# First chunk's keys and values as fp32 through POOL's queue, and a new order of the whole kernel

## The chip, the core and the metric

The kernel runs on one core of one Trainium2 chip. Five engines take part: TensorE (PE; matmuls and, through an identity matrix, transposes), VectorE (DVE), ScalarE (ACT), GpSimd (POOL) and SyncE (SP), which here only issues transfers. POOL issues transfers too. Each engine works through its own instructions in the order in which the program has them and waits on semaphores for the others. The metric is the device time of one execution in microseconds.

## What is computed

The reference has two stages. The first is a recurrence over 768 positions for 4 batches of 8 heads, each with a 48 x 48 state; the second a sum of four expert networks, weighted by row-normalised probabilities.

```python
f = 1.0 / (1.0 + np.exp(-f_logit))                     # q, k, v, f_logit: (4, 8, 768, 48)
for t in range(S):
    state = f[:, :, t, :, None] * state + np.einsum('bhd,bhe->bhde', k[:, :, t], v[:, :, t])
    y[:, :, t] = np.einsum('bhd,bhde->bhe', q[:, :, t], state)
x = y.transpose(0, 2, 1, 3).reshape(3072, 384)
p = domain_probs / (domain_probs.sum(-1, keepdims=True) + 1e-09)
for e in range(4):
    out += p[:, e:e + 1] * (np.maximum(x @ w1[e], 0.0) @ w2[e])   # w1: 384 x 1024, w2: 1024 x 384
```

## The kernel before

The 768 positions are cut into six chunks of 128. A chunk goes through the recurrence in its parallel form and then, batch by batch, into the four expert networks. Chunk 0 has no state before it, so it is the short way to the first expert matmul; everything below concerns it.

For each batch b of chunk 0 the steps are these, by the names that the code gives them:

- `gate1`, `gate2` (ScalarE, L334 and L339): log(1 + exp(-f)), the negative logarithm of the gate.
- `cs` and `cq` (TensorE, L351, L355 and L362): its running sums over the positions, by matmuls with triangular matrices.
- `exps` and `expq` (ScalarE, L382, L384 and L387): the exponentials of both sums, for the keys and for the queries.
- `k` and `q` (L397, L394): keys and queries multiplied by them, on VectorE or POOL.
- `tpk`, `tpq` (TensorE, L406) and `ev_tp` (L288): both are transposed and copied out of PSUM.
- `at` (TensorE, L437), `ev_at0` and `ev_at1` (L449 on VectorE with a 0/1 mask, or L445 on ScalarE with `mask1` on POOL, L441): the 128 x 128 products of keys and queries, with the future masked out.
- `y` (TensorE, L464), `ev_y` (L287 or L288): their product with v; `kv` (L470): the state for the next chunk.
- `xt` (TensorE, L490) and `ev_xt`: the transpose that the experts read. The expert matmuls `h` of chunk 0 (L499) follow, four blocks of 128 columns at a time for one batch.

v is needed in bf16 by `y` and `kv` (tile `vb`). In chunk 0 a transfer with a cast, issued on POOL (L293), writes `vb` directly; from chunk 1 on v is loaded as fp32 by SyncE and cast by POOL or ScalarE. Weights are always loaded with a cast, through POOL's queue (L312), in eleven pieces w0 to w10: w0 and w1 are the two halves of expert 0's first matrix. The loads of f, q and k of chunk 0 are issued by SyncE (L299 and L301), one of 192 KB for each batch. Ahead of chunk 1, its first loads of f are tied to the landing of weight pieces (`after(..., ins["w", w_gate])`).

All work is added to a plan as operations (`P.add`) with a cost on each engine, dependencies and buffers. A string of ranks, RANKS, has one number for each operation in the order in which they are added: the program is emitted in the order of these numbers, and a letter behind a number (A, D, P) puts an operation with a choice on ScalarE, VectorE or POOL. The costs and `free_at` in `Plan.run` only serve the choice of buffers; they wait for nothing on the chip. FILLER names operations ahead of which idle matmuls of 512 columns on a spare bank are put (L1156). SEQ is the order of POOL's issues, ORDER that of SyncE's adds, GATE makes an issue of v wait until keys have landed, and BYPOOL names the two masked evictions that ScalarE and POOL share.

Ahead of the plan stands a preparation that each engine runs first: an identity matrix, triangular matrices `Up`, `Wp` and `Ub`, the zeroed padding of tiles `gp`, `qk` and `e`, and the mask `mask01` (L193 to L230).

Of the kernel before, what the change touches and what calls it, by code (L numbers as in the profile page):

```python
# [11 lines left out]
ALU = mybir.AluOpType  # L12
# [79 lines left out]
class Plan:  # L92
# [20 lines left out]
    def run(self):  # L113
# [7 lines left out]
        for o in done:  # L121
            (e, cost), = o.costs.items()
            t = free_at[e]
# [1081 lines left out]
```

## Time and profile before

| | |
|---|---|
| median of three runs | 285.59 us (285.1 to 287.25) |
| the profiled execution | 285.82 us |
| its span in the trace | 284.1 us |
| TensorE busy | 276.0 us of the span, 97% |
| VectorE, ScalarE, POOL busy | 208.7, 178.2, 185.3 us |
| granted clock of TensorE | 1.00 in all stretches but the last |
| moved by the DMA engines | 41.88 MB, 147 GB/s on average |

In the views below, times count from the start of the span. A row of the timeline has start, length, engine, line, operation, output and inputs with their shapes, the number of instructions merged into the row, and in brackets the idle time of the engine before it with what ended it. A row of a table by stretches has the stretch, its length, the busy time of PE, PEld (its weight loads), DVE, ACT and POOL with the number of instructions, then the granted clock, the share of DMA time and GB/s. A row "DMA to landing" has the least, median and greatest time from the issue of a transfer to its landing, for the issues named in the row above it. The ends of matmuls are modelled, so a row of TensorE is a little longer than the time to the next one's start.

### The profile page before, as it was taken

To read this page: it belongs to the slowest core of one execution; us is meant where nothing else is said; L and a number is where in the kernel's file an instruction comes from. 1 tells how busy PE (TensorE), PEld (TensorE's weight loads), DVE (VectorE), ACT (ScalarE), POOL (GpSimd) and SP (SyncE) were. 2 spreads that over 40 slices of the span, in tenths; PEclk is the share of its full clock that TensorE was granted. 3 is DMA by queue.
4 is the path that set the end of the run, shared out by engine and by line. 5 is a ranking of instruction groups with operands and counts; after the bars stand their busy time and mean duration, and the time that the engine had idled before them with its cause. 6 is when DMAs were issued, how large, how long until landed. Compare 5 with 4: busy or idle time off the path is not lost.

```text
span 284.1 us, 8015 instructions
## 1 busy us (share of the span) xinstructions
PE 276.0 (97%) x3228; PEld 241.2 (85%) x3228; DVE 208.7 (73%) x437; ACT 178.2 (63%) x350; POOL 185.3 (65%) x197
## 2 busy tenths in 40 slices
PE   6889999999999999999999999999999999999995
PEld 4678565668788999999998999999999899999995
DVE  5695487797779587769887786686765687857683
ACT  5668235647898848686866867769367456556420
POOL 5799353706699878667729955695656545793761
PEclk9999999999999999999999999999999999999999
DMA  6999999999988999999999999996547015201003
GB/s 156 189 195 205 208 195 200 184 216 181 162 150 159 198 164 208 204 168 184 194 175 207 194 179 218 184 166 124 111 82 160 30 31 76 67 0 59 2 2 111
DMA packets 153688, 41.88 MB, mean 147 GB/s; under 512 B 144028, under 2 KB 152860, under 8 KB 153652
## 3 DMA queue, kind: packets, MB, share of 16 engines
q1 hardware_dynamic: 142404, 34.66, 65.1%
q0 software_dynamic: 11248, 6.72, 16.8%
q8 instruction: 25, 0.41, 0.6%
q14 instruction: 11, 0.09, 0.1%
HBM read 31.51 MB, written 4.72 MB: 128 GB/s over the span
## 4 chain that ended last, share of the span: by engine, by line
PE 84%; DMA 9%; POOL 4%; ACT 1%; DVE 1%; issue 0%; ACTq 0%; POOLq 0%
PE ps_m L646 29%; PE ps_m L531 26%; PE ps_m L574 7%; DMA w_sb<-in_moe_w_dram 7%; PE ps_m L514 6%; PE ps_m L499 4%; PE ps_m L654 2%; DMA f<-in_f_logit_dram 2%; PE ps_m L437 2%; POOL w_sb L312 2%; PE ps_m L464 1%; PE ps_m L460 1%; PE ps_m L347 1%; PE ps_m L470 1%; POOL AT L441 1%; PE ps_m L362 1%
## 5 line engine op out<-in xcount | busy, mean ns | idle before, releaser
L531 PE MATMUL ps_m<-x,w_sb 128*128 128x256 bf16 x672 | 84.3, 273 | 0.0
L531 PEld LDWEIGHTS <-w_sb 128*128 128x128 bf16 x672 | 63.6, 98 | 7.1
L595 ACT ACTIVATE h<-ps_m 128x512 bf16<-128x512 f32 x82 | 46.8, 600 | 24.1 <-PE ps_m L531 23.9
L646 PEld LDWEIGHTS <-S 128*128 128x128 bf16 x576 | 48.2, 98 | 0.8
L673 DVE TENSOR_TENSOR o<-ps_m,o 128x192 f32<-128x192 f32 x91 | 31.1, 353 | 19.1 <-PE ps_m L646 17.3
L646 PEld LDWEIGHTS <-h 128*128 128x128 bf16 x432 | 36.2, 98 | 0.8
L610 POOL TENSOR_TENSOR S<-h 128x1024 bf16<-128x1024 bf16 x14 | 29.7, 2124 | 10.3 <-DVE S L610 6.3
L499 PE MATMUL ps_m<-x,w_sb 128*128 128x128 bf16 (+2 forms) x264 | 35.1, 282 | 0.0
L420 ACT ACTIVATE yb<-ps_m,pn 128x384 bf16<-128x384 f32 x55 | 29.4, 586 | 8.5 <-PE ps_m L464 5.6
L397 POOL TENSOR_TENSOR qk<-q,e 128x384 bf16<-128x384 f32 x18 | 21.6, 1201 | 12.5 <-DVE f L549 3.9
L646 PE MATMUL ps_m<-ts_sb,S 128*128 128x192 bf16 x288 | 29.3, 246 | 0.0
L646 PE MATMUL ps_m<-w_sb,h 128*128 128x192 bf16 x288 | 29.2, 246 | 0.0
L646 PE MATMUL ps_m<-w_sb,S 128*128 128x192 bf16 x288 | 28.7, 246 | 0.0
L499 PEld LDWEIGHTS <-w_sb 128*128 128x128 bf16 x264 | 21.6, 98 | 8.1
L593 DVE TENSOR_SCALAR h<-ps_m 128x512 bf16<-128x512 f32 x30 | 20.6, 688 | 9.6 <-PE ps_m L531 8.5
L453 DVE TENSOR_TENSOR AT<-ps_m,mask 128x512 bf16<-128x512 f32 x40 | 25.6, 682 | 2.1 <-PE ps_m L437 2.0
L510 ACT ACTIVATE h<-ps_m 128x512 bf16<-128x512 f32 x33 | 19.1, 595 | 12.2 <-PE ps_m L499 11.8
L380 ACT ACTIVATE e<-ps_m 128x384 f32<-128x384 f32 x40 | 23.6, 708 | 3.2 <-PE ps_m L347 1.4
L610 POOL TENSOR_TENSOR S<-h,S 128x1024 bf16<-128x1024 bf16 x10 | 21.2, 2124 | 4.5 <-DVE o L673 2.5
L514 PE MATMUL ps_m<-w_sb,h 128*128 128x384 bf16 x128 | 23.9, 326 | 0.0
L585 DVE CUSTOM_DVE_ANT_0 h<-ps_m,QK 128x512 bf16<-128x512 f32 x24 | 16.0, 686 | 5.1 <-PE ps_m L574 1.9
L588 ACT COPY QK<-ps_m 128x512 f32<-128x512 f32 x24 | 13.8, 588 | 8.1 <-PE ps_m L574 5.2
(140 smaller groups left out, 523.3 us busy)
## 6 DMA issues: line engine op xcount, KB each, us to landing
out_dram<-o SPq DMA_DIRECT2D x23, 192.0 KB, 2.5
w_sb<-in_moe_w_dram POOLq DMA_DIRECT2D x5, 768.0 KB, 15.2
k<-in_k_dram SPq DMA_DIRECT2D x10, 384.0 KB, 5.1
q<-in_q_dram SPq DMA_DIRECT2D x10, 384.0 KB, 5.0
v<-in_v_dram SPq DMA_DIRECT2D x10, 384.0 KB, 5.1
f<-in_f_logit_dram SPq DMA_DIRECT2D x9, 384.0 KB, 5.8
w_sb<-in_moe_w_dram POOLq DMA_DIRECT2D x6, 384.0 KB, 8.2
f<-in_f_logit_dram SPq DMA_DIRECT2D x6, 192.0 KB, 4.4
```

The costliest lines, as they stand in the source:

```text
L380: nc.scalar.activation(out=o, in_=i, func=AF.Exp, scale=1.0 if j else -1.0)
L397: return engines[eng].tensor_tensor(out=tl("qk", c, b)[:, j, :, 0:D].rearrange("t (i r) d -> t i r d", r=2), in0=tl("qk"[j], c, b // 2)[:, ...
L420: nc.scalar.activation(out=ys, in_=y, func=AF.Copy, scale=pe)
L453: nc.vector.tensor_tensor(out=tl("AT", c, b)[:, r].rearrange("s i t -> s (i t)"), in0=tl("A", c, b, r).rearrange("s i t -> s (i t)"), in1= ...
L499: nc.tensor.matmul(out=hp(c, e, fc, n0, n1, nf)[:, f], lhsT=w1_sb[:, e, kk, (fc + f) * 128:(fc + f + 1) * 128], rhs=tl("xT", c)[:, kk, n0: ...
L514: nc.tensor.matmul(out=tl("op", c, e, nt)[:, 0:Din], lhsT=tl("h", c, e, half_of(c, nt * T))[:, fc, nt * T:(nt + 1) * T], rhs=w2_sb[:, e, f ...
L531: nc.tensor.matmul(out=out_[:, f], lhsT=w1_sb[:, e, kk, (fc + f) * 128:(fc + f + 1) * 128], rhs=tl("xs", c, hf, p)[:, el, kk, :], start=(k ...
L593: nc.vector.tensor_relu(out=dst, in_=tl("hp", c, hf, p, el, fc))
L595: nc.scalar.activation(out=dst, in_=tl("hp", c, hf, p, el, fc), func=AF.Relu)
L610: return engines[eng].tensor_tensor(out=o, in0=in0, in1=in1, op=op)
L646: nc.tensor.matmul(out=out_, lhsT=lhs[:, f, :], rhs=rhs[:, f, :], start=(first and el == 0 and f == 0), stop=(el == 1 and f == KH - 1), sk ...
L673: nc.vector.tensor_tensor(out=o, in0=src, in1=o, op=ALU.add)
```

## The change

Three things are changed in chunk 0 and in the preparation, and RANKS is another string for the whole kernel.

```diff
     def load(c, nm, b, n):
-        if (c, nm) == (0, "v"):
-            ins[c, nm, b] = nc.gpsimd.dma_start(out=tl("vb", c, b), in_=srcs[nm][c, :, b * H:(b + n) * H, :])
-            if f"v{b}" in GATE:
-                after(ins[c, nm, b], ins[GATE[f"v{b}"]])
+        if c == 0 and nm in "kv":
+            ins[c, nm, b] = nc.gpsimd.dma_start(out=tl(nm, c, b // 2)[:, hh(b, n), :], in_=srcs[nm][c, :, b * H:(b + n) * H, :])
             return
...
-        if x[0] == "v":
-            issued.append(P.add(f"v issue {i}", {"POOL": 0.8}, lambda _, i=i: load(0, "v", i, 1), -600 + 2 * j,
-                                deps=issued[-1:] + gate(x), takes=[("vb", 0, i)], lag=1.2))
+        if x[0] != "w":
+            issued.append(P.add(f"{x[0]} issue {i}", {"POOL": 0.95}, lambda _, i=i, nm=x[0]: load(0, nm, i, 1), -600 + 2 * j,
+                                deps=issued[-1:], takes=[(x[0], 0, i // 2)], lag=1.2))
...
-            vb = ld[0, "v", b] if c == 0 else P.add(f"v {c}.{b}", {"POOL": 0.52, "ACT": 0.54}, one(cast_v), s(4),
+            vb = P.add(f"v {c}.{b}", {"POOL": 0.52, "ACT": 0.54} if c else {"POOL": 0.52, "ACT": 0.54, "DVE": 0.34}, one(cast_v), s(4),
                        deps=[ld[c, "v", b]], takes=[("vb", c, b)], frees=[("v", c, half)])
...
-    nc.gpsimd.memset(Ub, 1.0)
-    nc.gpsimd.affine_select(out=Ub, in_=Ub, compare_op=ALU.is_ge, fill=0.0, base=0, channel_multiplier=-1, pattern=[[1, T]])
+
+    nc.vector.memset(Ub, 1.0)
+
+    def make_ub():
+        return nc.gpsimd.affine_select(out=Ub, in_=Ub, compare_op=ALU.is_ge, fill=0.0, base=0, channel_multiplier=-1, pattern=[[1, T]])
+
...
-        nc.gpsimd.memset(pads["e", i][:, 0:2 * NP * P2].rearrange("t (r d i) -> t r d i", r=2, i=NP)[:, :, D:P2, :], 0.0)
+        nc.vector.memset(pads["e", i][:, 0:2 * NP * P2].rearrange("t (r d i) -> t r d i", r=2, i=NP)[:, :, D:P2, :], 0.0)
     mask01 = const.tile([T, NP * T], BF16)
-    nc.gpsimd.memset(mask01, 1.0)
-    nc.gpsimd.affine_select(
-        out=mask01, in_=mask01, compare_op=ALU.is_ge, fill=0.0,
-        base=0, channel_multiplier=-1, pattern=[[0, NP], [1, T]],
-    )
+
+    nc.vector.memset(mask01, 1.0)
+
+    def make_mask():
+        return nc.gpsimd.affine_select(
+            out=mask01, in_=mask01, compare_op=ALU.is_ge, fill=0.0,
+            base=0, channel_multiplier=-1, pattern=[[0, NP], [1, T]],
+        )
+
...
+    masked = P.add("mask", {"POOL": 0.65}, lambda e: make_mask(), -599)
+    upper = P.add("ub", {"POOL": 0.3}, lambda e: make_ub(), -100)
...
-FILLER = {"cs 0.0": 6, "tpk 0.1": 4}
+FILLER = {"cs 0.0": 6, "y 0.1": 1, "y 0.0": 1}
...
-        free_at = {"DMA": 0.8, "DVE": 5.0, "POOL": 3.5, "ACT": 2.1, "PE": 2.0}
+        free_at = {"DMA": 0.8, "DVE": 6.0, "POOL": 2.9, "ACT": 2.1, "PE": 2.0}
...
-ORDER = "f0 k0 q0 f1 k1 q1 f2 f3 k2 q2 k3 q3"
-SEQ = "v0 v1 v2 w0 v3 w1"
+ORDER = "f0 q0 f1 q1 f2 f3 q2 q3"
+SEQ = "k0 k1 k2 v0 k3 v1 w0 v2 w1 v3"
 BYPOOL = "1.1 2.1"
 VW = (-2000, -480)
-GATE = {"v0": (0, "k", 1), "v1": (0, "k", 2)}
```

Keys and v of chunk 0 go as plain fp32 loads through POOL's queue, v is cast to `vb` by an operation of its own, POOL's part of the preparation ends with `Up` (the fills go to VectorE, the two selections become operations of the plan), and nothing waits by GATE any more. `masked` is a dependency of the evictions of `at`, `upper` of the running sums of later chunks.

What the two strings of ranks make of the first stage, read off for each queue and engine (batch numbers behind the names, "a" and "b" for the halves of batch 3):

| | before | after |
|---|---|---|
| SyncE's loads | f0 f1 k2 f2 k1 k0 q0 q1 q2 f3 k3 q3 probabilities | f0 q0 f1 q1 f2 f3 q2 probabilities q3 |
| POOL | issues of v0 v1 v2 w0 v3; k 2; issues of w1 w2; mask1 of 1; issues of w3 w4 w5; mask1 of 2; issue of w6 | issues of k0 k1 k2 v0 k3 v1 w0; ub; issue of v2; mask; cast v 0; issue of w1; mask1 of 1; issues of v3 w2; mask1 of 2; cast v 2; issues of w3 to w8 |
| ScalarE | gate1 0, gate2 0, gate1 1, gate2 1, exps 0, gate1 2, exps 1, expq 1, gate2 2, expq 0, expq 2, exps 2, gate1 3, gate2 3, ev_at1 1, exps 3, expq 3, ev_y 0 | gate1 0, gate2 0, gate1 1, gate2 1, gate1 2, expq 0, exps 0, gate2 2, expq 1, exps 1, expq 2, exps 2, gate1 3, gate2 3, ev_tp 0, ev_at1 1, cast v 1, expq 3, exps 3, ev_y 1, ev_y 0 |
| VectorE | k 1, k 0, q 0, q 1, ev_tp 0, q 2, ev_tp 1, ev_at0 0, ev_at1 0, ev_at0 1, ev_tp 2, k 3, q 3, ev_kv 0, ev_at0 2 | q 0, k 0, q 1, k 1, q 2, k 2, ev_tp 1, ev_tp 2, ev_at0 1, ev_at1 0, ev_at0 0, q 3, k 3, ev_xt 1, ev_tp 3a, ev_at0 2 |
| TensorE | cs 0, cq 0, cs 1, cq 1, tpk 1, cq 2, tpk 0, cs 2, tpq 0, tpq 1, at 0, tpq 2, at 1, cs 3, cq 3, tpk 2, y 0, kv 0, at 2, xt 0, y 1, tpk 3, tpq 3, probabilities, kv 1, first h (batch 0) | cs 0, cq 0, cq 1, cs 1, cq 2, cs 2, tpk 0, tpq 1, tpq 0, tpk 1, tpq 2, tpk 2, cq 3, at 1, at 0, probabilities, cs 3, at 2, y 1, y 0, kv 0, xt 1, tpq 3, tpk 3, xt 0, first h (batch 1) |

More of the change, by code (lines that the diff above doesn't have):

```diff
@@ L312, in load_w @@
         ins["w", i] = nc.gpsimd.dma_start(out=w[:, e, ks, cols], in_=r[e][:, ks, cols])
-        if f"w{i}" in GATE:
-            after(ins["w", i], ins[GATE[f"w{i}"]])
         if i == w_last:
@@ L689 @@
     issued, late = [], {(0, x[0], int(x[1])): i for i in LATE for x in LATE[i].split()}
-    def gate(x):
-        return [ld[GATE[x]]] if x in GATE else []
     for i, x in enumerate(ORDER.split()):
-        add_load(0, x[0], int(x[1]), 1, -1000 + i)
+        add_load(0, x[0], int(x[1]), 1, -1000 + i, deps=[o for o in P.ops[-1:] if i])
     every = slice(0, None)
@@ L704 @@
         i = int(x[1:])
-        if x[0] == "v":
-            issued.append(P.add(f"v issue {i}", {"POOL": 0.8}, lambda _, i=i: load(0, "v", i, 1), -600 + 2 * j,
-                                deps=issued[-1:] + gate(x), takes=[("vb", 0, i)], lag=1.2))
-            ld[0, "v", i] = P.add(f"ld v0.{i}", {"DMA": 1.45}, lambda _: None, VW[0] + j, deps=issued[-1:] + fifo[-1:], lag=2.0)
-            fifo.append(ld[0, "v", i])
+        if x[0] != "w":
+            issued.append(P.add(f"{x[0]} issue {i}", {"POOL": 0.95}, lambda _, i=i, nm=x[0]: load(0, nm, i, 1), -600 + 2 * j,
+                                deps=issued[-1:], takes=[(x[0], 0, i // 2)], lag=1.2))
+            ld[0, x[0], i] = P.add(f"ld {x[0]}0.{i}", {"DMA": 0.6}, lambda _: None, VW[0] + j, deps=issued[-1:] + fifo[-1:], lag=2.0)
+            fifo.append(ld[0, x[0], i])
             continue
@@ L717 @@
         iss = P.add(f"w issue {i}", {"POOL": 0.8}, lambda _, i=i, x=(e, which, ks, cols): load_w(i, *x),
-                    -600 + 2 * j, deps=issued[-1:] + gate(x) + ([ld[1, "k", 0]] if i == w_last else []), lag=1.5)
+                    -600 + 2 * j, deps=issued[-1:] + ([ld[1, "k", 0]] if i == w_last else []), lag=1.5)
         op = P.add(f"w {i}", {"DMA": 1.95 if i < 6 else 4.05}, lambda _: None, -400 if i == w_last else (VW[1] if i < 2 else -480) + j, deps=[iss] + fifo[-1:], lag=1.0)
@@ L754, in attention @@
             cs = P.add(f"cs {c}.{b}", {"PE": 0.165 if c else 0.45}, on(pe_cs), s(0),
-                       deps=[G[b]], takes=[pt_("cs")], lag=0.2, frees=[("gp", c, half)])
+                       deps=[G[b]] + ([upper] if c else []), takes=[pt_("cs")], lag=0.2, frees=[("gp", c, half)])
             ex = P.add(f"exps {c}.{b}", {"ACT": 1.19 if c else 0.56}, on(exps), s(0) + 0.1, deps=[cs],
@@ L794, in attention @@
             at, vb = AT_[b], VB[b]
-            eA = [P.add(f"ev_at{r} {c}.{b}", {"ACT": 0.735} if c == 0 and f"{b}.{r}" in BYPOOL.split() else {"DVE": 0.685 if c else 0.73}, one(ev_at, r), s(7) + 0.1 + 0.1 * r, deps=[at],
+            eA = [P.add(f"ev_at{r} {c}.{b}", {"ACT": 0.735} if c == 0 and f"{b}.{r}" in BYPOOL.split() else {"DVE": 0.685 if c else 0.73}, one(ev_at, r), s(7) + 0.1 + 0.1 * r, deps=[at, masked],
                         takes=[("AT", c, b)], frees=[pt_("A", r)]) for r in range(2)]
```

123 rows, old and new, of the table RANKS are left out of this document.

## The prediction

> **What bounds the kernel now.** The page comes first, then TensorE's busy time in stretches of 10 us, because a mean over the span does not say where the little idle time lies.
>
> ```profile
> span 284.1 us, 8015 instructions
> PE 276.0 (97%) x3228; PEld 241.2 (85%) x3228; DVE 208.7 (73%) x437; ACT 178.2 (63%) x350; POOL 185.3 (65%) x197
> ```
> ```profile
> 0.00:10.00 10.00, 7.78 (x40) 4.65 (x41) 5.24 (x16) 6.18 (x13) 5.86 (x20) 1.00 0.77 177
> 10.00:20.00 10.00, 7.92 (x129) 6.64 (x128) 8.22 (x17) 6.37 (x15) 9.33 (x11) 1.00 1.57 180
> 20.00:30.00 10.00, 10.00 (x143) 7.91 (x138) 5.14 (x15) 7.29 (x14) 9.54 (x20) 1.00 1.25 207
> ...
> 40.00:50.00 10.00, 9.32 (x75) 6.29 (x73) 7.64 (x17) 4.78 (x8) 4.50 (x3) 1.00 1.13 196
> ...
> 280.00:284.10 4.10, 0.99 (x13) 0.77 (x10) 0.78 (x3) 0.00 (x0) 0.00 (x0) 0.97 0.38 135
> ```
> The second number of each row is TensorE's busy time. Of its 8.1 us of idleness 2.2 and 2.1 lie in the first 20 us, 0.7 between 40 and 50, and 3.1 behind its last matmul. From 20 us on TensorE is the bound, so the change is worth what it does to the moment at which the unbroken stretch begins, and to the one wait at about 48 us. Busy is not useful, though: the timeline of TensorE shows fillers and slow matmuls in the first stage.
>
> ```profile
> 4.96 0.80 PE L351 MATMUL ps_m<-gp,Up 128*128 128x192 bf16 x4 [0.70 <-POOL mask L220]
> ...
> 7.68 1.92 PE L1156 MATMUL ps_m<-S 128*128 128x512 bf16 x4
> ...
> 10.85 0.49 PE L351 MATMUL ps_m<-gp,Up 128*128 128x192 bf16 x4
> ...
> 18.89 0.83 PE L499 MATMUL ps_m<-x,w_sb 128*128 128x128 bf16 x12
> ```
> L1156 are the fillers, which fill waits. Four equal matmuls of L351 take 0.80 us at 4.96 and 0.49 at 10.85, so TensorE reaches its speed only at about 10.8 us. The first expert matmul (L499) starts at 18.89, and from there the end of the kernel is a sum of matmuls.
>
> **Part by part.** The first question is what ScalarE gets when. Its rows, with SyncE's issues and the size of one load:
>
> ```profile
> 4.39 0.53 ACT L339 ACTIVATE gp<-f 128x384 bf16<-128x384 f32 x1
> ...
> 6.70 0.52 ACT L334 ACTIVATE f<-f 128x384 f32<-128x384 f32 x1 [0.27 <-DMA f<-in_f_logit_dram]
> ...
> 7.99 0.49 ACT L387 ACTIVATE e<-ps_m 128x384 f32<-128x384 f32 x1 [0.17 <-PE ps_m L362]
> 8.38 0.52 ACT L339 ACTIVATE gp<-f 128x384 bf16<-128x384 f32 x1
> 8.79 0.48 ACT L387 ACTIVATE e<-ps_m 128x384 f32<-128x384 f32 x1
> ```
> ```profile
> 2.92 0.61 SPq L299 DMA_DIRECT2D f<-in_f_logit_dram  x1
> ...
> 3.57 1.45 SPq L301 DMA_DIRECT2D k<-in_k_dram  x2
> ```
> ```profile
> w_sb<-in_moe_w_dram POOLq DMA_DIRECT2D x6, 384.0 KB, 8.2
> f<-in_f_logit_dram SPq DMA_DIRECT2D x6, 192.0 KB, 4.4
> ```
> ```profile
> 4.00:10.00 6.00, 5.30 (x35) 3.77 (x34) 2.62 (x5) 4.73 (x12) 2.99 (x5) 1.00 1.04 232
> 10.00:18.00 8.00, 5.92 (x100) 4.88 (x97) 6.80 (x13) 5.29 (x13) 7.33 (x8) 1.00 1.60 177
> ```
> *SyncE's queue.* The ranks put its loads as f0, q0, f1, q1, f2, f3, q2, the probabilities, q3. In ScalarE's new order the third gate (f2) stands ahead of every exponential (gate1 of 2 has rank 21, the first exponential 22), so nothing of batch 0 goes on before f2 has landed; call that time T. Before, f2 was fourth and landed at 6.70. As fifth it comes one load later: 0.65 us by the spacing of the issues (2.92 to 3.57), 0.85 by 192 KB at 232 GB/s, so about 7.4. Now the keys come through POOL's queue beside it. None of k0 ahead of f2's bytes gives T = 7.4, all of k0 and k1 ahead gives 7.4 + 1.7 = 9.1. I take 8.2, one load's worth, since POOL can start k0 only after its masks, as follows.
>
> ```profile
> 1.76 1.04 POOL L202 TENSOR_SCALAR_AFFINE_SELECT Up<-par 128x128 bf16<-128x128 bf16 x4 [0.39 <-DVE par L197]
> ...
> 4.29 0.63 POOL L220 TENSOR_SCALAR_AFFINE_SELECT mask<-mask 128x512 bf16<-128x512 bf16 x1
> ...
> 7.87 2.85 POOL L293 DMA_DIRECT2D vb<-in_v_dram  x3 [2.94 <-DMA k<-in_k_dram]
> ```
> The Trainium skill (DMA: Bandwidth & Descriptors, "Issuing engines are not separate DMA queues") speaks against the split: transfers started by several engines run on the same 16 DMA engines and interleave, and only issue time is saved. By that rule the 1.5 loads that SyncE's queue still has at that point (q1 and f2) let 1.5 loads of keys pass, T would be 7.4 + 1.3 = 8.7, and the result 0.5 us above my sum; the rows lean to it, with 232 GB/s from one queue (4 to 10 us) and 177 from two (10 to 18, where one of them casts).
>
> *From T to the first expert matmul.* ScalarE starts an instruction about 0.4 us after the one before (7.99, 8.38, 8.79). Gate, expq 0, exps 0, second gate of batch 2: the fourth starts at T + 1.25 and ends at T + 1.8. The cumulative sums cq 2 and cs 2 follow on TensorE, twice 0.80 at the slow speed, and exps 2 takes 0.5: T + 3.9. The rest is VectorE's order, k 2, the evictions of transposes 1 and 2, three masked evictions, q 3, k 3, the eviction of x 1:
>
> ```profile
> 4.59 0.36 DVE L230 CAST ident<-ident 24x24 f32<-24x24 bf16 x1
> ...
> 13.37 1.97 DVE L449 TENSOR_TENSOR AT<-ps_m,mask 128x512 bf16<-128x512 f32 x3
> ...
> 15.24 0.67 DVE L288 COPY QK<-ps_m 112x1024 bf16<-112x1024 bf16 x1
> ...
> 16.29 0.56 DVE L394 TENSOR_TENSOR qk<-q,e 128x384 bf16<-128x384 f32 x1
> ...
> 19.93 0.36 DVE L288 COPY x<-ps_m 128x384 bf16<-128x384 bf16 x1
> ```
> That is 3 x 0.56 + 2 x 0.67 + 1.97 + 0.36 = 5.35, so T + 9.25 if VectorE never waited. It does wait for transposes and attention products on TensorE; I allow 0.4 with TensorE at speed and 1.2 without (the 0.80 against 0.49 above, over some four such groups), and take 0.75. The first expert matmul starts at T + 10.0 = 18.2, against 18.89: 0.7 us gained, with bounds of T + 9.65 = 17.05 (1.85 gained) and 9.1 + 10.45 = 19.55 (0.65 lost). The work done on TensorE by then is the same as before but for kv 1 (one group), which I leave out.
>
> *The weights.* What must cover this is w0.
>
> ```profile
> L312 POOL DMA_DIRECT2D w_sb<-in_moe_w_dram x1: 768/768/768, 10.7 to 10.7; - x1
> ...
> DMA to landing us min/median/max: 8.0/8.0/8.0
> ```
> ```profile
> L312 POOL DMA_DIRECT2D w_sb<-in_moe_w_dram x1: 809/809/809, 14.0 to 14.0; - x1
> ...
> DMA to landing us min/median/max: 7.3/7.3/7.3
> ```
> ```profile
> L293 POOL DMA_DIRECT2D vb<-in_v_dram x4: 893/918/1077, 7.9 to 11.4; - x4
> ...
> DMA to landing us min/median/max: 6.1/7.1/8.4
> ```
> Those are w0, w1 and the four loads of v. Before, w0 landed at 10.7 + 8.0 = 18.7, with the first expert matmul right behind it, and w1 at 14.0 + 7.3 = 21.3. The four cast loads of v landed between 7.9 + 6.1 = 14.0 and 11.4 + 8.4 = 19.8; with w0 among them (384 KB at 207 GB/s, 1.9 us), three took 5.8 - 1.9 = 3.9 us, 1.3 each, where a plain load took 0.85. In the new order fourteen plain loads are ahead of w0; with f0 in at about 3.8 (before the first gate, which ended where the second begins, 4.39), 13 x 0.85 + 1.9 puts w0 at 16.8 and w1, behind v2, at 19.5. So w0 has 1.4 us in hand. All later weights should come some 1.3 us earlier too (four times 0.45 of cast saved, less a gap while v3 and w2 stand behind the mask of batch 1 in POOL's order).
>
> *The wait at 48 us.*
>
> ```profile
> 47.24 0.84 ACT L334 ACTIVATE f<-f 128x768 f32<-128x768 f32 x1 [1.47 <-DMA f<-in_f_logit_dram]
> ```
> The gate of the second chunk waits for a load that is itself tied to a weight's landing. TensorE arrives 0.7 us earlier, the load up to 1.3, so up to 0.6 of the 0.7 us of idleness goes; I take half, 0.35.
>
> *What costs nothing.* POOL's mask work ended at 4.29 + 0.63 = 4.92, and the first sum waited for it, but the gate that it also needs ended at 4.39 + 0.53 = 4.92: no gain. VectorE takes over the fills; its preparation ended at 4.95 and its first product now comes at T + 0.9, a cover of 4 us. The masks are made on POOL behind eight issues of 0.95 (2.85 / 3), by about 11.5, and are needed at T + 6. Two casts of v lie on POOL (before, it idled 2.9 us there) and two on ScalarE, which VectorE's order outlasts. They add waits: behind the cast of v0 on POOL stand w1's issue and the mask of batch 1, behind that of v1 on ScalarE expq 3 and the evictions of y 1 and y 0; v0 and v1 should be in at 3.8 + 9 x 0.85 = 11.5 and 3.8 + 13 x 0.85 = 14.9, about when POOL and ScalarE (T + 7) come to them. The removed fillers filled waits; their only price would be the clock, below.
>
> Sum: the profiled execution took 285.82 (span 284.1, the rest around it; the median of the runs shown is 285.59). 285.82 - 0.7 - 0.35 = **284.8 us**.
>
> **Rivals.**
> *Both queues together carry more* (T = 7.4, TensorE at speed): start at 17.05, 1.85 gained, and the wait at 48 gone, 0.7: 283.2. For it: v's cast loads made the mixed stage slow. Against it: one queue alone already moved 232 GB/s.
> *The clock stays down.* Before, TensorE sped up at 10.8 after work without a break since 4.96, in which the four fillers at 7.68 (1.92 us) closed a gap. These fillers go, and between the sums of batch 1 (about 8) and those of batch 2 (T + 1.8 = 10) nothing runs. If TensorE then needs the same 5.9 us of dense work, and finds it only among the expert matmuls, half of it is lost, 2.9, and the start slips by the other 0.45 of its allowance: 284.8 + 3.35 = 288.2. It decides where the first twelve matmuls of L499 take about 1.5 us in place of 0.83. Against it: sums, transposes and products between T + 1.8 and T + 7 are dense at the low speed and may raise it earlier. The Trainium skill (TensorE: Matmul & The Clock Gate, "What's actually happening") gives a free-running window of about 3.4 us; by that the loss is half of 3.4, and the time 287.0.
> *Packets of POOL's queue stay dear without the cast*, 1.3 us a load: w0 lands at 16.8 + 6 x 0.45 = 19.5 and w1 at 19.5 + 7 x 0.45 = 22.7, 1.4 us later than before, and everything behind it with it: 285.82 + 1.4 = 287.2. It decides from about 1.1 us a load (18.2, where the sum has the first expert matmul). For it: all that the trace shows of v's loads. Against it: the cast goes, and a load then writes what a load of SyncE's writes.
>
> **Chances.** Forecast 0.40, both queues 0.27, clock 0.22, dear packets 0.11. One per cent is about what a measurement here can tell (the three runs span 285.1 to 287.25). Faster by over 1% is under 282.7: the first rival with a little more from the new order elsewhere, 0.18. Slower by over 1% is above 288.4: the clock's upper half, and clock and packets together, 0.22. Within: 0.60. The range runs from 282.5 (the first rival and 0.7 us of order) to 288.7 (the clock and half a microsecond). The forecast's own range, with T half a load off, the wait wholly gone or wholly kept and TensorE's allowance at either end, is 283.7 to 286.0.
>
> **What would show it.** Right: gate1 of f2 at about 8.2 with ScalarE waiting for that load; L499 first at about 18.2 and not waiting for w0; no wait near 48 of over 0.4. Wrong: L499 ended by a wait for a weight (packets), x12 of L499 above 1.2 us (clock), L499 ahead of 17.3 (both queues), or new idle stretches of TensorE after 20 us, which would mean that the new order, not the loads, decides.

## The result, and the profile after

The kernel after took 293.78 us (median of four runs, 293.48 to 294.8), the kernel before on the same chip 285.79 (285.1 to 287.25): a ratio of 1.0279 with a 95% interval of 1.0231 to 1.0326. That is 8 us slower, where the prediction had 284.8 us and a range up to 288.7. Each ratio in this document compares undisturbed runs alone, so it can differ a little from the quotient of the medians beside it.

The page of the kernel after, its first lines, and TensorE's busy time in the first three stretches (the second number of each row):

```profile
span 292.0 us, 8002 instructions
...
PE 278.3 (95%) x3226; PEld 243.1 (83%) x3226; DVE 213.3 (73%) x448; ACT 179.5 (61%) x353; POOL 186.1 (64%) x191
```
```profile
0.00:10.00 10.00, 5.81 (x30) 3.50 (x31) 4.64 (x19) 4.61 (x10) 8.94 (x19) 1.00 0.80 186
10.00:20.00 10.00, 6.28 (x60) 5.39 (x59) 5.00 (x10) 5.06 (x14) 2.44 (x5) 0.84 0.77 157
20.00:30.00 10.00, 9.54 (x157) 8.26 (x157) 7.92 (x19) 6.25 (x16) 7.88 (x11) 0.82 0.91 142
```
From 10 to 20 us TensorE does 60 matmuls, where the kernel before does 129 in the same stretch, and every engine is less busy than before: something outside them is awaited. The chain of waits names it. Here are its longest pieces (start, length, what) in order of time, those of TensorE left out:

```profile
4.96 11.18 DMA q<-in_q_dram
...
54.35 10.55 DMA v<-in_v_dram
...
108.34 2.06 POOL S L615
110.40 3.43 DMA egs<-e
```
The queries of batch 2 are issued at 4.96 us and land at 16.14. The timeline shows what stands behind them. First ScalarE and VectorE, then TensorE and POOL, each row with its idle time and its cause in brackets:

```profile
8.77 0.52 ACT L339 ACTIVATE f<-f 128x384 f32<-128x384 f32 x1 [2.15 <-DMA f<-in_f_logit_dram]
...
16.23 0.56 DVE L399 TENSOR_TENSOR qk<-q,e 128x384 bf16<-128x384 f32 x1 [4.13 <-DMA q<-in_q_dram]
```
```profile
16.85 1.07 PE L411 MATMUL ps_m<-ident,qk 128*128 128x128 bf16 x8 [3.15 <-DVE qk L399]
...
24.23 0.83 PE L504 MATMUL ps_m<-x,w_sb 128*128 128x128 bf16 x12
```
```profile
17.32 0.51 POOL L297 CAST vb<-v 128x384 bf16<-128x384 f32 x1 [6.11 <-DVE qk L402]
17.77 0.77 POOL L319 DMA_DIRECT2D w_sb<-in_moe_w_dram  x1
```
f2 lands at about 8.7, inside the bounds of the forecast, and the third gate starts at 8.77. VectorE goes through q 0, k 0, q 1 and k 1 and then stands 4.13 us for q 2, with its evictions queued behind; TensorE's transposes of batch 2 wait for VectorE. POOL's first cast of v is tied to VectorE's k 2 (the plan lets products and casts of the two engines take turns, and makes each turn a wait), so POOL stands 6.11 us although v0 landed at about 12.3, and w1's issue, which follows in its queue, comes at 17.77 where it came at 13.97 before. The first expert matmul (L504, before L499) starts at 24.23: 5.3 us later than before.

The wait for q 2 is 4.13 us of that. Behind it TensorE is slow, and VectorE waits for it twice more:

```profile
19.20 1.95 DVE L454 TENSOR_TENSOR AT<-ps_m,mask 128x512 bf16<-128x512 f32 x3 [0.55 <-PE ps_m L442]
...
20.06 0.82 PE L356 MATMUL ps_m<-gp,Up 128*128 128x192 bf16 x4
...
23.79 0.36 DVE L297 COPY x<-ps_m 128x384 bf16<-128x384 bf16 x1 [1.71 <-PE ps_m L495]
```
```profile
18.00:20.00 2.00, 2.00 (x24) 1.49 (x22) 1.45 (x3) 0.83 (x2) 0.56 (x2) 0.50 0.15 19
```
Four sums take 0.82 us at 20.06, where the kernel before needs 0.49 from 10.85 on, and the granted clock from 18 to 20 us is 0.50 (the third number from the end of the last row). So the two waits, 2.3 us together, come on top of the one for q 2.

The later start is two thirds of the loss. The rest lies behind the first expert matmul. TensorE's share of that stretch, before and after (stretch, its length, busy time):

```profile
18.89:284.10 265.21, 261.42 (x3087) 1.00 0.80 145
```
```profile
24.23:292.00 267.77, 261.96 (x3087) 1.00 0.79 143
```
The same matmuls take 2.6 us longer: 0.5 more in busy time, 2.0 in idle time (5.8 against 3.8). The waits, added up by cause (total, times, longest):

```profile
PE ps_m L536 <- ACT e L385: 1.3, 1, 1.3
PE ps_m L469 <- POOL vb L297: 0.4, 1, 0.4
PE ps_m L442 <- DVE AT L454: 0.3, 1, 0.3
PE ps_m L495 <- ACT yb L296: 0.2, 1, 0.2
```
The wait at 48 us of before (0.7) is gone, as hoped, but 2.2 us of others stand for it. The largest is at 114 us: an exponential of chunk 3 waits until its tile `e` is free, because the copy of the decay factors of chunk 2, batch 3 (`egs`), still reads it. POOL issues this copy at 110.40 behind a sum of 2.1 us (L615), as the last two rows of the chain show; L615 adds up hidden values of the experts, though two expectations below call it a state sum. In these profiles the 2.6 us are thus 1.5 more of waits (2.2 against 0.7), 0.5 more behind the last matmul (3.6 against 3.1) and 0.5 more of busy time.

### The profile page after: what moved, and what is told of

Same layout as the page of the kernel before. It is cut to its first block, busy times and chain, and to the rows that moved or that the text cites. A ratio compares the mean times of both kernels' runs of the same rounds, so it can differ in the third digit from the quotient of the medians.

```text
span 292.0 us, 8002 instructions
## 1 busy us (share of the span) xinstructions
PE 278.3 (95%) x3226; PEld 243.1 (83%) x3226; DVE 213.3 (73%) x448; ACT 179.5 (61%) x353; POOL 186.1 (64%) x191
## 4 chain that ended last, share of the span: by engine, by line
PE 74%; DMA 17%; POOL 3%; DVE 2%; SPq 1%; issue 1%; ACT 1%; POOLq 0%; DVEq 0%; ACTq 0%
PE ps_m L651 27%; PE ps_m L536 23%; PE ps_m L579 7%; DMA w_sb<-in_moe_w_dram 6%; DMA q<-in_q_dram 4%; PE ps_m L504 4%; DMA v<-in_v_dram 4%; PE ps_m L519 4%; PE ps_m L442 2%; DMA f<-in_f_logit_dram 2%; PE ps_m L469 2%; PE ps_m L659 1%; POOL w_sb L319 1%; SPq L306 1%; PE ps_m L465 1%
## 5 line engine op out<-in xcount | busy, mean ns | idle before, releaser
L536 PE MATMUL ps_m<-x,w_sb 128*128 128x256 bf16 x672 | 83.2, 273 | 1.3 <-ACT e L385 1.3
L600 ACT ACTIVATE h<-ps_m 128x512 bf16<-128x512 f32 x79 | 45.7, 598 | 33.4 <-PE ps_m L536 28.9
L615 POOL TENSOR_TENSOR S<-h 128x1024 bf16<-128x1024 bf16 x14 | 30.1, 2150 | 10.9 <-ACT h L600 5.1
L504 PE MATMUL ps_m<-x,w_sb 128*128 128x128 bf16 (+2 forms) x264 | 35.3, 282 | 0.0
L425 ACT ACTIVATE yb<-ps_m,pn 128x384 bf16<-128x384 f32 x52 | 28.0, 582 | 3.7 <-DVE yb L427 2.2
L504 PEld LDWEIGHTS <-w_sb 128*128 128x128 bf16 x264 | 21.6, 98 | 8.6 <-issue 0.2
L598 DVE TENSOR_SCALAR h<-ps_m 128x512 bf16<-128x512 f32 x33 | 22.1, 685 | 6.8 <-PE ps_m L536 6.7
L615 POOL TENSOR_TENSOR S<-h,S 128x1024 bf16<-128x1024 bf16 x9 | 19.2, 2129 | 7.8 <-DVE S L615 7.7
L402 POOL TENSOR_TENSOR qk<-q,e 128x384 bf16<-128x384 f32 x17 | 20.2, 1194 | 2.4 <-DVE qk L402 0.8
L593 ACT COPY QK<-ps_m 128x512 f32<-128x512 f32 x24 | 13.9, 588 | 12.2 <-PE ps_m L579 5.8
L515 ACT ACTIVATE h<-ps_m 128x512 bf16<-128x512 f32 x31 | 17.4, 601 | 6.1 <-PE ps_m L504 5.1
```

What stands on the lines that cost most here:

```text
L425: nc.scalar.activation(out=ys, in_=y, func=AF.Copy, scale=pe)
L504: nc.tensor.matmul(out=hp(c, e, fc, n0, n1, nf)[:, f], lhsT=w1_sb[:, e, kk, (fc + f) * 128:(fc + f + 1) * 128], rhs=tl("xT", c)[:, kk, n0: ...
L536: nc.tensor.matmul(out=out_[:, f], lhsT=w1_sb[:, e, kk, (fc + f) * 128:(fc + f + 1) * 128], rhs=tl("xs", c, hf, p)[:, el, kk, :], start=(k ...
L598: nc.vector.tensor_relu(out=dst, in_=tl("hp", c, hf, p, el, fc))
L600: nc.scalar.activation(out=dst, in_=tl("hp", c, hf, p, el, fc), func=AF.Relu)
L615: return engines[eng].tensor_tensor(out=o, in0=in0, in1=in1, op=op)
```

## The experiments

Theory A: the fp32 loads of keys and v go through POOL's queue in large packets, the loads of SyncE's queue in small ones, the DMA engines serve the queues packet by packet, and so SyncE's q 2 starves; the late q 2 delays the first expert matmul. Theory B: the new order itself is worse, wherever the loads go. Rivals: the queue of POOL behind the cast (w1 late), and the clock (removed fillers).

### q 2 through POOL's queue

```diff
-            ins[c, nm, b] = nc.sync.dma_start(out=tl(nm, c, b // 2)[:, hh(b), :].rearrange("t (h j) d -> t h (j d)", j=2), in_=src)
+            ins[c, nm, b] = (nc.gpsimd if (nm == "q" and b in (2,)) else nc.sync).dma_start(out=tl(nm, c, b // 2)[:, hh(b), :].rearrange("t (h j) d -> t h (j d)", j=2), in_=src)
...
-    done = P.run()
+    done = sorted(P.run(), key=lambda o: MOVE.get(o.name, o.prio))
...
+MOVE = {'ld q0.2': 5.5}
```
MOVE gives single operations of the plan another place in the emitted order; here q 2 stands behind POOL's issue of k 2.

> The changed kernel, with the one load of q for batch 2 issued by POOL behind the third load of keys instead of by SyncE. Theory (SyncE's queue is starved beside POOL's fp32 loads, so q 2 lands at 16.1 us and VectorE waits 4.1 us for it): q 2 lands at about 12.4, where v 0 landed; VectorE's wait of 4.1 us goes; the first expert matmul (L504) comes at 20 to 21 us instead of 24.2; the time is 289 to 290.5. Rival (the new order of the engines is to blame, and q 2 only happened to be last): something else is late in its place, L504 stays above 23, the time above 292.

Measured: 288.42 us (286.39 to 290.22), before 285.53, ratio 1.0099 (1.0067 to 1.0131). TensorE's timeline:

```profile
20.38 0.83 PE L504 MATMUL ps_m<-x,w_sb 128*128 128x128 bf16 x12
```
One load put into the other queue brings the first expert matmul 3.85 us forward and the time 5.4 down (5.1 by the ratios), a little more than was expected. TensorE is at speed in time here, and VectorE hardly waits for it:

```profile
17.58 0.51 PE L356 MATMUL ps_m<-gp,Up 128*128 128x192 bf16 x4
...
19.97 0.36 DVE L297 COPY x<-ps_m 128x384 bf16<-128x384 bf16 x1 [0.16 <-PE ps_m L495]
```
The late q 2 is the cause of the late start; 1% remains. That it is late because of the packets, this run doesn't show.

### The transfers of before under the new order

```diff
-            ins[c, nm, b] = nc.gpsimd.dma_start(out=tl(nm, c, b // 2)[:, hh(b, n), :], in_=srcs[nm][c, :, b * H:(b + n) * H, :])
+            if nm == "k":
+                ins[c, nm, b] = nc.sync.dma_start(out=tl(nm, c, b // 2)[:, hh(b, n), :], in_=srcs[nm][c, :, b * H:(b + n) * H, :])
+            else:
+                ins[c, nm, b] = nc.gpsimd.dma_start(out=tl("vb", c, b), in_=srcs[nm][c, :, b * H:(b + n) * H, :])
...
     def cast_v(c, b, eng):
+        if c == 0:
+            return None
```
SyncE's loads are then f0 f1 f2 q0 k0 q1 k1 q2 k2 f3 q3 k3, and v is cast by its transfer, as before the change; v0 and v1 again wait for the landing of keys 1 and 2. The changed preparation and fillers stay.

> The changed kernel in its new order, but with the transfers of the kernel before: keys by SyncE, v cast on its way by POOL and tied to the landing of keys 1 and 2; the four casts of v on chip are left out. Theory (the transfers cost most, the new order behind 24 us some 2 us): L504 at 18.5 to 19.5, the time 286.5 to 288.5. Rival (the new order is the cause): L504 above 22, the time above 291.

Measured: 288.93 us (288.13 to 290.49), ratio 1.0101 (1.0046 to 1.0157). TensorE's timeline (this file has L511 for the first expert matmul), and its waits behind it:

```profile
19.00 0.83 PE L511 MATMUL ps_m<-x,w_sb 128*128 128x128 bf16 x12
```
```profile
PE ps_m L543 <- ACT e L390: 1.6, 1, 1.6
PE ps_m L476 <- POOL vb L297: 1.6, 1, 1.6
```
The start is level with before (18.89), and the kernel is still 1% slower. So B holds for a part: about 3 us (1.3 to 4.5 by the interval) belong to the order with its preparation and fillers, with no load of keys or v through POOL as fp32. The time is 0.4 above the range that was expected. Its two waits are the same two places as in the kernel after: the `egs` copy, and `y` of chunk 1 waiting for the cast of a v that lands late.

### The weight issues ahead of the cast

```diff
+MOVE = {'w issue 1': 56.5, 'v issue 3': 56.6, 'w issue 2': 56.7}
```

> The changed kernel with the issues of w1, v 3 and w2 moved ahead of the cast of v 0 in POOL's order, so that they no longer stand behind POOL's wait of 6.1 us for VectorE. Theory (the weights are late but nobody waits for them): w1 is issued at about 11 and lands near 19 instead of 22.4, the DMA engines are not empty between 17 and 19.5, the first L504 stays at 24 (within 0.5, or later where q 3 is starved as well), the time stays within 1 of 293.8. Rival (late weights are the price of the change): the time falls by 2 to 4.

Measured: 292.45 us (291.38 to 293.15), ratio 1.0217 (1.0176 to 1.0258); the first expert matmul:

```profile
24.36 1.31 PE L504 MATMUL ps_m<-x,w_sb 128*128 128x128 bf16 x12
```
The weights are there early now, and the first expert matmul does not move. POOL's held-up queue was a consequence and not the cause; the time falls by 1.3 us, but the intervals of the two ratios overlap. The twelve matmuls take 1.31 us here, above the 1.2 that the prediction had named as the sign of the clock: in this run TensorE is slow until about 25 us.

### The queues by themselves

A kernel of transfers alone (loads, and zeros as the result): six loads of 192 KB by SyncE in the shape of q and f, six by POOL in the shape of k, plain and with a cast, each alone and then both queues together; last, SyncE's beside four weight loads.

> Transfers alone, none of the computation, the output is zeros: six phases, each begun when the one before has landed. Six loads of SyncE alone (192 KB each, 384 B pieces); six fp32 loads of POOL alone (192 KB, 192 B pieces); six cast loads of POOL alone (the same to bf16); six of SyncE beside six fp32 of POOL; six of SyncE beside six cast of POOL; six of SyncE beside four weight halves with a cast. Theory (POOL's fp32 pieces travel as packets of about 4 KB and the engines change queues by packets): beside fp32 loads the later loads of SyncE take 3 to 4 us each against 0.9 alone; beside cast loads 1.5 to 2. Rival (queues share bytes evenly): 1.7 to 2 each in both. POOL's fp32 load alone: 0.8 to 1.0 us by the theory that the cast was dear, 1.3 or more by the rival that POOL's packets are dear in themselves.

The packets of each queue while it is alone, first SyncE's, then POOL's plain loads, then its cast loads (packets, MB, share of engine time):

```profile
q1 hardware_dynamic: 3168, 1.18, 57.3%
```
```profile
q0 software_dynamic: 384, 1.18, 54.0%
```
```profile
q0 software_dynamic: 6240, 0.59, 141.5%
```
1.18 MB make 3168 packets of about 370 bytes on SyncE's queue and 384 of about 3,100 on POOL's; with a cast POOL writes 0.59 MB in 6240 packets of 95 (their times overlap, so the share passes 100%). Alone, the cast loads are not dear: their issues at POOL, 0.9 us each, set the pace of both kinds. The fourth load of SyncE's six, from issue to landing, alone, beside plain loads of POOL, beside cast loads, beside weights:

```profile
DMA to landing us min/median/max: 3.2/3.2/3.2
```
```profile
DMA to landing us min/median/max: 9.2/9.2/9.2
```
```profile
DMA to landing us min/median/max: 6.6/6.6/6.6
```
```profile
DMA to landing us min/median/max: 12.5/12.5/12.5
```
Any neighbour delays SyncE's load, the plain one by 6.0 us, the cast one by 3.4. The direction is that of A. The size is not: the six loads together take 12.2 us beside plain loads and 11.2 beside cast ones, 2.0 and 1.9 each, which is what the rival of even bytes had expected, and only the fourth stands out. This run alone doesn't decide between packets and bytes. POOL's own loads, 3.2 to 4.0 us from issue to landing when alone, take 4.4 to 6.4 beside SyncE's when plain and 6.1 to 8.7 with a cast.

### Small packets in the changed kernel

The targets of k and v are declared as float32r, an fp32 type of the same size, and POOL's queue then leaves the loads in pieces of 192 bytes. The queue, the number of bytes and the order stay.

```diff
-            ins[c, nm, b] = nc.gpsimd.dma_start(out=tl(nm, c, b // 2)[:, hh(b, n), :], in_=srcs[nm][c, :, b * H:(b + n) * H, :])
+            ins[c, nm, b] = nc.gpsimd.dma_start(out=tl(nm, c, b // 2)[:, hh(b, n), :].bitcast(mybir.dt.float32r), in_=srcs[nm][c, :, b * H:(b + n) * H, :])
```

> The changed kernel; the keys and v of chunk 0 take the same queue, order and bytes, but their target is declared as float32r, so that the transfer counts as one with a cast and should not be put together into packets of about 4 KB. Theory (the turns of the queues go by packets): SyncE's loads get far more of the turns, q 2 lands at 11 to 14 instead of 16.1, VectorE's wait for it shrinks from 4.1 to under 1.5, the first expert matmul (L504) comes at 20 to 22, the time is 288 to 290.5. Rival (the bytes ahead of q 2 decide, whatever their packets): q 2 at 16, the time within 1 of 293.8.

Measured: 290.38 us (288.5 to 291.86), before 286.35, ratio 1.011 (1.0037 to 1.0182). The queues from 9 to 12 us, in the kernel after and here:

```profile
q0 software_dynamic: 156, 0.50, 72.0%
q1 hardware_dynamic: 524, 0.21, 42.5%
```
```profile
q0 software_dynamic: 1677, 0.32, 103.3%
q1 hardware_dynamic: 922, 0.38, 71.3%
```
With the packets small, SyncE's queue gets 0.38 MB in these 3 us in place of 0.21, and POOL's 0.32 in place of 0.50. The loads of f3 and q2, from issue to landing, after and here, and then the first expert matmul here:

```profile
DMA to landing us min/median/max: 7.5/9.4/11.2
```
```profile
DMA to landing us min/median/max: 6.0/6.5/7.0
```
```profile
19.55 0.83 PE L504 MATMUL ps_m<-x,w_sb 128*128 128x128 bf16 x12
...
28.41 0.82 PE L504 MATMUL ps_m<-x,w_sb 128*128 128x512 bf16 x3 [0.97 <-DMA w_sb<-in_moe_w_dram]
```
q 2 lands at 12.0, the wait of VectorE for it is gone, and the first expert matmul is 4.7 us earlier, by an edit that leaves the queues and the bytes as they are. That bears A out for the start. A part comes back as a wait for a weight at 28 us, as the weights' issues still follow the cast on POOL. One thing stays mixed: the Trainium skill (DMA: Bandwidth & Descriptors, "SWDGE vs HWDGE vs iDMA") counts a float32r target as a cast. The packets are what the rows show to differ; that a cast by itself helps SyncE was not tested apart from them.

The Trainium skill (DMA: Bandwidth & Descriptors, "Queues, rings and completion order") says that each DMA engine goes round its queues and drains a whole packet before it switches. These runs agree: the queue with the larger packets gets more of the bytes. They show no exchange of one packet for one, though, since SyncE passed 524 packets to POOL's 156; whether both queues had work on every DMA engine all the time isn't shown.

### The two misplaced transfers

The order of the run with the transfers of before, with v of batches 0 and 1 of chunk 1 issued ahead of f of batches 2 and 3 of that chunk (the "second f" of the expectation), and the `egs` copy ahead of the sum of L615:

```diff
+MOVE = {..., 'ld v1.0': 258.5, 'egs 2.3': 573.5}
```

> The new order with the old transfers (as in e2_old_transfers), with two operations moved forward: the load of v of chunk 1 ahead of the second load of f of chunk 1 on SyncE, and the transfer of the decay factors of chunk 2, batch 3, ahead of the state sum that precedes it on POOL. Theory (what the new order costs behind the first stage are two waits of TensorE, 1.7 us at 59 and 1.75 at 109): both go, the time is 285 to 286.3, about that of the kernel before. Rival (the order is slower all along, the waits only show it): one or both come back elsewhere, the time stays above 287.5.

Measured: 289.11 us (286.57 to 290.97), before 286.35, ratio 1.0092 (1.0056 to 1.0129): a miss. Two of TensorE's waits, the first of them at 61 us:

```profile
PE ps_m L357 <- ACT gp L352: 1.1, 1, 1.1
...
PE ps_m L543 <- ACT e L390: 0.3, 1, 0.3
```
The wait for `egs` fell from 1.6 to 0.3. The wait for v did not go, it changed its name: whichever load is issued beside the last weight at 49 us takes 11 us to land, and when that is f and no longer v, the gate of chunk 1 is late. Both are due by 61 us in this order. In the kernel before this f takes as long (10.5 us, issued at 48.64), but TensorE doesn't wait for it there.

### The same two moves, q 2 through POOL, f first

```diff
+MOVE = {'ld q0.2': 5.5, 'ld v1.0': 258.5, 'egs 2.3': 573.5, 'ld f0.1': 0.1, 'ld f0.2': 0.2, 'ld q0.0': 0.3, ...}
```

> The changed kernel with q 2 through POOL's queue (as in e1_q2_through_pool), the two moves of e5_old_transfers_two_moves, and SyncE's loads in the order f0 f1 f2 q0 q1 f3, so that f 2 is through before POOL's large packets begin. Theory: f 2 lands at about 5.6 instead of 10.1, the first expert matmul comes at 18 to 19 instead of 20.4, and the two waits at 61 and 111 go: 284.5 to 286.5. Rival (the first stage is bound by the bytes of POOL's queue, k 2 and q 2): the first expert matmul stays above 19.5, the time above 286.5.

Measured: 289.24 us (287.61 to 291.41), ratio 1.0113 (1.0078 to 1.0148), a miss too. The first expert matmul, and TensorE's largest wait behind it:

```profile
19.88 0.83 PE L504 MATMUL ps_m<-x,w_sb 128*128 128x128 bf16 x12
```
```profile
PE ps_m L352 <- ACT gp L347: 2.1, 2, 1.6
```
The third gate starts 4.2 us earlier than in the first experiment (5.91 against 10.14), and the start gains 0.5 us: q 2, at 12.1, was hardly earlier (12.5 there), and TensorE was slow again, with a granted clock of 0.50 from 14 to 18 us. TensorE then waits for gates of chunk 1 at 50 and 61 us.

### The kernel before without the fillers

```diff
-FILLER = {"cs 0.0": 6, "tpk 0.1": 4}
+FILLER = {"cs 0.0": 6}
```

> The kernel before without its four fillers ahead of the transposes of batch 1. Theory (the clock is a small part): TensorE reaches its speed at some point before 14 us all the same, the first expert matmul moves by under 0.5 us, the time stays within 1 of 285.5. Rival (the removed fillers are what the change lost): TensorE is still slow at the first expert matmuls, twelve of L499 take above 1.2 us, the time rises by 2 or more.

Measured: 286.69 us (285.07 to 289.26), before 286.35, ratio 0.9987 (0.9944 to 1.003). In the kernel before, the fillers are worth nothing that can be measured; about the clock in the changed kernel this run says nothing.

### All repairs together, and an attempt on the kernel before

Small packets, the weight issues ahead of the cast, and the two moves, in the changed kernel:

```diff
+MOVE = {'w issue 1': 56.5, 'v issue 3': 56.6, 'w issue 2': 56.7, 'ld v1.0': 258.5, 'egs 2.3': 573.5}
```

> The changed kernel with all repairs together: POOL's loads of keys and v in small packets, the issues of w 1, v 3 and w 2 ahead of the first cast of v on POOL, the load of v of chunk 1 ahead of the second f, and the copy of the gate sums of chunk 2 ahead of the state sum on POOL. Theory (late q 2 and the POOL queue behind it are the start's loss, two misplaced transfers the loss in the middle, and 1 to 2 us are the new order's own): first expert matmul at 19 to 20 us, no wait for a weight at 27 us, none above 0.6 us at 111, a wait of about 1.3 us left at 61, time 286.5 to 288.5 beside a before of 285.6 to 286.4. Rival (the small packets keep the DMA engines longer, so what SyncE gains POOL loses): the first weights land after 20 us, a wait for them of 1 us or more stays, and the time is that of the small packets alone, 289.5 to 290.5.

Measured: 288.31 us (287.54 to 290.34), before 285.93, ratio 1.009 (1.006 to 1.012). Its timeline, its largest wait, one piece of its chain of waits, and the stretch behind the first expert matmul:

```profile
18.69 0.83 PE L504 MATMUL ps_m<-x,w_sb 128*128 128x128 bf16 x12
```
```profile
PE ps_m L352 <- ACT gp L347: 1.6, 2, 0.8
```
```profile
49.79 10.29 DMA f<-in_f_logit_dram
```
```profile
18.69:286.60 267.91, 261.81 (x3083) 1.00 0.80 144
```
The start is 0.2 us ahead of before, no weight is waited for, `egs` is gone from the list, and the stretch behind still takes 267.9 us against 265.2. The start is repaired; the rest is the order's own, of which the gates of chunk 1 show 1.6 us (0.7 before) and the time behind the last matmul 0.5 more than before.

The kernel before waits for a gate of chunk 1 as well, at 48 us. There the load of f that it needs was let go one weight earlier:

```diff
         if (c, nm, b) == (1, "f", 1):
-            after(ins[c, nm, b], ins["w", w_gate])
+            after(ins[c, nm, b], ins["w", w_gate - 1])
+        if (c, nm, b) == (1, "k", 0):
+            after(ins[c, nm, b], ins["w", w_gate])
```

> The kernel before, with one wait changed: the second load of f of chunk 1, which waits for the ninth weight load (issued at 41.45 us, landed at 47.15), waits for the eighth (landed 36.57) instead, and the keys behind it on SyncE's queue keep the wait for the ninth. If the wait of TensorE at 48 us (0.68 us, for a gate of chunk 1) is only this late landing, f lands at about 43, the wait goes, the two last weight loads land up to 1 us later, and the time is 0.3 to 0.8 us below the kernel before. If the DMA engines are full in this stretch whatever the order, the wait moves to a weight or to the keys and the time stays within 0.3 us.

Measured: 286.63 us (285.29 to 288.21), before 285.93, ratio 1.0011 (0.9978 to 1.0044). The load, and TensorE's wait:

```profile
L301 SPq DMA_DIRECT2D f<-in_f_logit_dram x1: 367/367/367, 36.6 to 36.6; - x1
...
DMA to landing us min/median/max: 10.1/10.1/10.1
```
```profile
PE ps_m L349 <- ACT gp L344: 0.9, 1, 0.9
```
Issued 4.9 us earlier, it lands 0.45 us earlier: beside two weights it takes 10.1 us in place of 5.7. The wait stays, and a weight is waited for 0.4 us besides. No version was found that beats the kernel before.

## Why the prediction was wrong

- **T, the landing of f2, 8.2 with bounds 7.4 and 9.1.** Inside the bounds: about 8.7. That is the value which followed from the rule on interleaved queues that the prediction cited, but partly by luck: between 3 and 8.7 us POOL's queue moved 0.43 MB, some 2.2 loads in place of 1.5, and both queues together 251 GB/s in place of 232. The steps up to the exponential of batch 2, T + 3.9, were right too: it ended at 12.63.
- **"From T to the first expert matmul", T + 10.0.** This step failed. It counted VectorE's instructions on the condition that VectorE never waits for a transfer, and never asked when q 2, the seventh load on SyncE's queue, lands. It landed at 16.14, VectorE stood 4.13 us, and the first expert matmul came at T + 15.5. With q 2 in time, the step holds: T + 10.3 with q 2 through POOL (f2 at 10.1, matmul at 20.38), T + 10.8 with small packets alone, T + 10.2 with all repairs (f2 at 8.5, matmul at 18.69). So the missing term was a transfer. A second term was too small: the sum allowed 0.75 us, at most 1.2, for VectorE's waits for TensorE, and the changed kernel has 2.3, since TensorE is slow there until past 23 us. The prediction's T + 9.25 without waits, 4.1 and 2.3 make T + 15.6.
- **How the queues share.** Behind that failed step stands the picture of two queues that give each other load for load. By it f3 and q 2 and two loads of POOL's follow f2 at 0.85 us each, and q 2 lands at about 12.1 (an estimate from the prediction's own terms), just when VectorE asks for it. The packets go with another share: POOL's plain loads have some 3,100 bytes in each, SyncE's 370, and at 9 to 12 us POOL's queue moved 0.50 MB to SyncE's 0.21; with small packets, q 2 lands at 12.0.
- **"TensorE is the bound from 20 us on", so that only the start and the wait at 48 us count.** Failed as well, for 2.6 us. The wait at 48 did go, and others came: for v or f of chunk 1 and for `egs`. With the start repaired, the kernel stays 0.9% slower (0.6 to 1.2%). The prediction named new idle stretches behind 20 us as what would refute it, but gave them no price.
- **The weights.** w0 was forecast at 16.8 and landed at 16.6. w1 was forecast at 19.5 and landed at 22.35, as its issue stood behind the cast of v0, which stood behind VectorE. The prediction named that queue but had the cast wait for v0 alone, and overlooked its tie to VectorE's turn. It cost the start nothing: with w1 ahead of the cast, the first expert matmul is where it was.
- **Cast loads dear, 1.3 us against 0.85.** Not when alone: there POOL's issues of 0.9 us pace both kinds. Beside SyncE's loads the cast ones are slower, 6.1 to 8.7 us from issue to landing against 4.4 to 6.4, and v's loads in the kernel before took 6.1 to 8.4.
- **Rivals.** Both queues carry more: no, T was 8.7 and not 7.4, and VectorE's wait shows the reverse for SyncE's. The clock: not by its mark, since twelve matmuls of L504 took 0.83 us. But it was down for nearly the whole first stage, and this has a price: T + 15.5 less the 4.1 for q 2 is T + 11.4, against T + 10.2 to T + 10.8 where q 2 is in time, so some 0.6 to 1.2 us (an estimate from these runs) of the 5.3. In the three runs with q 2 in time TensorE was at speed by 14 to 17 us, without any of the fillers that the change removed; so its slowness here goes with the gap of 3.15 us in which it waits for q 2, but no run holds q 2 back and the clock up, or the reverse. Dear packets of POOL's queue: no by its mark, since w0 landed at 16.6 and not at 19.5; the packets matter, but it is SyncE's loads that they delay.

The account by the two profiled spans, 292.0 against 284.1: 5.3 us at the start (the wait for q 2, and the slow TensorE behind it) and 2.6 behind it (the order and its waits), together 7.9. One execution has an uncertainty of its own: the kernel before without fillers took 266.9 us behind its first expert matmul. So it is the ratios of the runs with a repaired start, 1.009 to 1.011, that carry the second term. What of the new order makes it, beyond the waits that are named, was not settled; putting the old ranks under the new transfers was not tried.

## What to carry to other kernels

Before transfers are moved to another queue, look at the packet counts of both queues: in these runs a queue of large packets took bytes from a queue of small ones, and a later load of the weak queue showed it. For each load ask who stands in line behind its first reader, in program order, on that engine. A searched order is only as good as its model of transfers: a load of 5 us that takes 11 beside a weight can turn into a wait wherever the search has put it.

## What the runs showed of the hardware

- The loads of k and v with 192-byte pieces went out as packets of about 3,100 bytes through POOL's queue when plain, and as many small ones (95 bytes with a cast; ten times as many packets as float32r, 1677 for 0.32 MB against 156 for 0.50). SyncE's queue left its pieces of 384 bytes apart (packets of 370 to 410 bytes).
- Beside POOL's weight loads one SyncE load took 12.5 us, against 3.2 alone and 9.2 beside plain loads of keys. The four weight loads move more bytes than the six of keys, so this isn't a comparison for equal bytes.
- The fillers of the kernel before bring TensorE to speed earlier, and it is worth nothing that can be measured. Without them its groups of four sums (L351) still take 0.82 us at 13.96, where 0.49 stood at 10.85 already; the time is the same. With the old transfers under the new order, which has no such fillers either, the third group (L361) is at speed at 8.59 already:

```profile
13.96 0.82 PE L351 MATMUL ps_m<-gp,Up 128*128 128x192 bf16 x4
```
```profile
8.59 0.49 PE L361 MATMUL ps_m<-gp,Up 128*128 128x192 bf16 x4
```
